# Attention out of its branch, one branch for the expert slots with the usual arm laid last (RWKV attention with top-1 experts, one Trainium2 core)

## The chip, the cores and the metric

The kernel runs on one core of a Trainium2 chip. The metric is the time of one execution on the device in microseconds (us), the median of several runs. Engines are called PE (TensorE), DVE (VectorE), ACT (ScalarE), POOL (GpSimd) and SP (SyncE); each runs its own program, and a branch stands in all five programs.

## The reference

An RWKV attention over 4 batches, 8 heads, 768 tokens of 48 elements, and then a layer of 8 experts, of which each of the 3072 tokens takes the best one (384 elements in, 1024 between).

```
for t in range(S):
    cur = einsum('bhd,bhe->bhde', u * k[t], v[t])
    y[t] = einsum('bhd,bhde->bhe', r[t], state + cur)
    state = w[:, :, None] * state + einsum('bhd,bhe->bhde', k[t], v[t])
x = y, as 3072 x 384
logits = x @ w_gate;  e_idx = argmax(logits)
gate_w = softmax(logits)[e_idx];  eom = sigmoid(x @ w_output_gate)
for e in range(8):
    h = maximum(x[e_idx == e] @ w1[e], 0)
    out[e_idx == e] = gate_w * eom[:, e] * (h @ w2[e])
```

w lies between 0.85 and 0.95 in the inputs that are timed.

## The kernel before

**Head.** Constants are made, w and u are loaded by `load_heads` on SP's queue (four small loads), and r, k and v of the first chunks too. `make_flag` and `read_flag` find out whether all w are between 0.6 and 1.6; the result is `flag`, read into a register of each engine at line 1178. `make_powers` computes powers of w for one chunk.

**Attention.** It is computed in 24 chunks of 128 tokens. That holds for w near 1; the branch at line 1234 on `flag` has this chunked form as its first arm (the fall-through), and in its second arm `slow_attention`, which goes token by token. `Attention.first` transposes r and k of the first chunk (`ps_f`) and multiplies them by the powers (`RT`, `KT`), `prep` multiplies those of later chunks (`Rn`, `Kn`), `product` makes `P`. While PE works on chunk i, the router works on chunk i - 1 and finds each token's expert and its place in it. The order of all instructions in this part is that of the code (`manual_schedule`). After the arm's last instruction each engine jumps over the other arm; the place where they meet is called the join here.

**Experts.** Expert slots 0 to 7 are worked one after the other. A slot has two layers: `l1` (lines 799 to 801, three products of high and low halves in fp32r, into `ps_h`; `l1_out` makes `hh` on ACT and `hl` on DVE from it) and layer 2 (`l2_step`, lines 861 to 863, into `ps_o`). `gather` (line 770, an indirect DMA on POOL) fetches a slot's tokens into `xg`; `xt` (line 782) transposes them into `ps_xt` and splits them. `split1` and `split2` split weights into halves, `load1` and `load2` fetch the next ones. `scatter` scales the rows (`yo`) and writes them with an indirect DMA on POOL (line 836). The first 256 columns of slot 0 are worked at the end of the attention (`early_rest`), the other 256 behind the join: `run` orders their eight pieces of `l1` by hand, with the rest of the router's last work among them (among it the small table `ps_tab`); then `layer2(0, ...)`, outside the manual order, so that a scheduler places its matmuls, and the gathers' transposes and the weights of slot 1 with them.

**Levels.** How many rows of each expert are computed is a table, `CAPS[n]`. `level` (line 905) is a branch on the number that the router found: level 0 is the usual one and the first arm (the fall-through); two more arms follow, and behind the first one each engine jumps over them. Last, at line 1368, a branch on `ovf` around `overflow`, which computes tokens that found no place; here it has none.

The functions that the change touches:

Of the kernel before, what the change touches and what calls it, by code (L numbers as in the profile page):

```python
# [19 lines left out]
C = 128  # L20
# [26 lines left out]
WARM = (4, 0, 0, 0, 1, 3)  # L47
# [157 lines left out]
class Attention:  # L205
    def __init__(self, tc, ctx, k, load, x_d):
        self.tc, self.k = tc, k
        self.load, self.x_d = load, x_d
        self.pw = ctx.enter_context(tc.tile_pool(name="att_w", bufs=2))
        self.T = None  # L210
        self.st, self.vc, self.A = {}, {}, [None, None]
        self.Rn, self.Kn = ([self.pw.tile([C, H, HB], F32, name=f"{nm}{i}", bufs=1) for i in range(n)] for nm, n in (("Rn", 2), ("Kn", 3)))
# [12 lines left out]
    def first(self, ps):  # L225
        nc, k = self.tc.nc, self.k
        ts = self.load(0)
        RK = [None, None]
        for n in (1, 0):
            p = ps.tile([C, NP, C], F32, name="ps_f", tag="at", bufs=2)  # L230
            warm_up(self.tc, k, WARM[2 + n])
            for q in range(NP):
                nc.tensor.transpose(p[:, q, :], k.raw0["rk"[n]][:, 2 * q : 2 * q + 2, :], k.ident)
            RK[n] = self.pw.tile([C, NP, C], F32, name=("RT", "KT")[n])
            nc.vector.tensor_mul(RK[n], p, (k.pr, k.pk)[n])
        self.st[0] = [None, None, ts[2]] + RK

    def product(self, i):
# [3 lines left out]
        self.P = self.pw.tile([C, NP, C], F32, name="P", bufs=1)  # L242
# [15 lines left out]
    def trans(self, ps, i):  # L258
# [4 lines left out]
        RT = self.pw.tile([C, NP, C], F32, name="RT")  # L263
        KT = self.pw.tile([C, NP, C], F32, name="KT")
# [78 lines left out]
class Router:  # L343
    def __init__(self, tc, pool, k, wg, wog):
# [22 lines left out]
        self.level = pool.tile([1, 1], I32, name="level")  # L367
        self.ovf = pool.tile([1, 1], I32, name="ovf")
# [315 lines left out]
    def finish(self, w, tot):  # L684
# [28 lines left out]
        yield V  # L713
        nc.vector.tensor_copy(self.level, lvl)


class Experts:
    def __init__(self, tc, ctx, k, rt, w1, w2, x_d, out):
# [8 lines left out]
        self.xg = [p.tile([QP, DM], F32, name=f"xg{q}") for q in range(NQ)]  # L727
        self.ys, self.ph = {}, {}
# [98 lines left out]
    def scatter(self, s, q, p, pool=None):  # L827
        nc = self.tc.nc
        n = self.rows(s, q)
        yo = (pool or self.op).tile([QP, DM], F32, name=f"yo{q}")  # L830
# [44 lines left out]
    def early_rest(self, ps, pool):  # L875
# [5 lines left out]
        for q in range(EARLY):  # L881
# [7 lines left out]
            self.scatter(0, q, p, pool)  # L889
        self.gather(1, range(self.nq(1)))  # L890

    def run(self, rest):
        with self.tc.manual_schedule(engines=ORDERED):
            for f in range(FC):
# [500 lines left out]
```

## Time and profile before

| | |
|---|---|
| median of 3 runs | 400.09 us (400.07 to 401.25) |
| profiled execution | 400.7 us |
| its span | 399.0 us |
| granted clock of PE, mean | 0.981 |

The span is the time from the first to the last instruction of the profiled execution; 1.7 us of its time lie outside. All times of rows count from the span's start. A granted clock of 1.00 is 2.4 GHz, and 0.50 is 1.2 GHz.

### The profile page before, as it was taken

The page shows a single profiled execution, that of the slowest core. Times are in us where ns is not written, and L with a number is a line of the kernel's source. Part 1 is how long each engine was busy: PE and PEld are TensorE (multiplying, and loading weights), DVE is VectorE, ACT ScalarE, POOL GpSimd, SP SyncE. Part 2 cuts the span into 40 slices and gives each one's busy share as a digit, 9 for nine tenths or more (in the row PEclk, how much of TensorE's full clock was granted, in tenths as well). Part 3 has the DMA queues.
Part 4 walks back from the last instruction along what each step waited for, and adds up shares of the span by engine and source line. Part 5 has one row for each costly group of instructions (what it writes and reads, how often), then busy time and mean ns, then how long its engine had stood idle before and what let it go on. Part 6 is the DMA issues. An engine that isn't in the chain of part 4 may idle for free. (4 is left out here: it accounts for less than half of the span.)

```text
span 399.0 us, 12122 instructions
## 1 busy us (share of the span) xinstructions
PE 368.8 (92%) x5004; PEld 350.6 (88%) x5004; DVE 229.8 (58%) x516; ACT 150.5 (38%) x303; POOL 122.0 (31%) x170
## 2 busy tenths in 40 slices
PE   6899999999898989689999999999999999999960
PEld 3799989998787888689989999999999999999960
DVE  5776797678888648347651652662654636625200
ACT  2233323333243452134542652653634626525200
POOL 6423234232346772241501331232224216010020
PEclk9999999999999999979999999999999999999995
DMA  7976776775987320743371751751852935620010
GB/s 124 189 153 143 164 151 131 160 161 121 222 216 185 102 81 2 222 134 120 120 245 39 221 178 46 220 176 50 257 162 77 284 106 166 209 82 17 2 60 5
DMA packets 104970, 54.87 MB, mean 138 GB/s; under 512 B 78911, under 2 KB 102515, under 8 KB 104896
## 3 DMA queue, kind: packets, MB, share of 16 engines
q1 hardware_dynamic: 101472, 44.08, 42.9%
q0 software_dynamic: 3424, 9.82, 7.5%
q8 instruction: 44, 0.72, 0.8%
q14 instruction: 30, 0.25, 0.2%
HBM read 44.45 MB, written 9.76 MB: 136 GB/s over the span
## 5 line engine op out<-in xcount | busy, mean ns | idle before, releaser
L799 PE MATMUL ps_h<-xh,w1h 128*128 128x384 f32 (+4 forms) x216 | 73.5, 340 | 4.7 <-issue 4.1
L800 PE MATMUL ps_h<-xl,w1h 128*128 128x384 f32 (+4 forms) x216 | 71.7, 332 | 0.0
L801 PE MATMUL ps_h<-xh,w1l 128*128 128x384 f32 (+4 forms) x216 | 71.7, 332 | 0.0
L836 POOL DMA_INDIRECT out_dram<-yo,si x28 | 28.8, 1028 | 135.0 <-ACT yo L833 72.8
L243 POOL TENSOR_TENSOR P<-RT,KT 128x512 f32<-128x512 f32 x24 | 30.8, 1283 | 72.7 <-ACT xT L379 45.2
L809 DVE SCALAR_TENSOR_TENSOR hl<-ps_h,hh 128x384 fp32r<-128x384 f32 (+4 forms) x72 | 37.9, 532 | 18.1 <-ACT hh L808 17.7
L808 ACT ACTIVATE hh<-ps_h 128x384 fp32r<-128x384 f32 (+4 forms) x72 | 33.9, 473 | 37.8 <-PE ps_h L801 36.0
L799 PEld LDWEIGHTS ps_h<-xh,w1h 128*128 128x128 f32 x216 | 41.8, 194 | 5.7 <-issue 4.4
L770 POOL DMA_INDIRECT xg<-x_d,gi x28 | 31.2, 1114 | 45.8 <-PE ps_xt L782 30.0
L861 PE MATMUL ps_o<-w2h,hh 128*128 128x384 f32 x128 | 43.5, 340 | 0.0
L863 PE MATMUL ps_o<-w2h,hl 128*128 128x384 f32 x128 | 42.9, 335 | 0.0
L862 PE MATMUL ps_o<-w2l,hh 128*128 128x384 f32 x128 | 42.8, 334 | 0.0
L800 PEld LDWEIGHTS ps_h<-xl,w1h 128*128 128x128 f32 x216 | 41.8, 194 | 0.1
L801 PEld LDWEIGHTS ps_h<-xh,w1l 128*128 128x128 f32 x216 | 41.7, 193 | 0.2
L748 DVE TENSOR_TENSOR w1l<-raw,w1h 128x768 fp32r<-128x768 f32 x28 | 26.7, 955 | 22.8 <-ACT w1h L747 22.8
L285 DVE TENSOR_TENSOR A<-ps_a,mask 128x512 f32<-128x512 f32 x48 | 30.8, 683 | 10.1 <-PE ps_a L281 9.9
L747 ACT CAST w1h<-raw 128x768 fp32r<-128x768 f32 (+1 forms) x36 | 27.1, 763 | 25.1 <-PE ps_h L800 20.0
L785 DVE TENSOR_TENSOR xl<-ps_xt,xh 128x384 fp32r<-128x384 f32 (+4 forms) x27 | 13.6, 536 | 30.5 <-ACT xh L784 30.2
L748 DVE TENSOR_TENSOR w2l<-raw,w2h 128x768 fp32r<-128x768 f32 x28 | 26.7, 960 | 7.4 <-ACT w2h L747 5.7
L269 ACT COPY KT<-ps_t 128x512 f32<-128x512 f32 x23 | 13.5, 587 | 44.0 <-PE ps_t L268 40.6
L747 ACT CAST w2h<-raw 128x768 fp32r<-128x768 f32 (+1 forms) x36 | 26.9, 764 | 7.2 <-PE ps_o L863 2.8
L281 PE MATMUL ps_a<-RT,KT 64*64 64x128 f32 x768 | 26.9, 276 | 0.9 <-DVE vc L255 0.8
(217 smaller groups left out, 698.0 us busy)
## 6 DMA issues: line engine op xcount, KB each, us to landing
raw<-in_moe_w_dram SPq DMA_DIRECT2D x64, 384.0 KB, 3.6
x_d<-x SPq DMA_DIRECT2D x24, 192.0 KB, 3.6
v_t<-in_v_dram SPq DMA_DIRECT2D x21, 192.0 KB
k_t<-in_k_dram SPq DMA_DIRECT2D x20, 192.0 KB, 3.6
r_t<-in_r_dram SPq DMA_DIRECT2D x20, 192.0 KB, 4.2
raw<-in_v_dram SPq DMA_DIRECT2D x3, 192.0 KB, 3.6
raw<-in_k_dram SPq DMA_DIRECT2D x3, 192.0 KB, 3.1
xg<-x_d,gi POOLq DMA_INDIRECT x28, 4.4
```

The source lines that it names most:

```text
L243: self.tc.nc.gpsimd.tensor_mul(self.P, RT, KT)
L747: nc.scalar.copy(hi, self.raw[i][:, cs])
L748: (eng or nc.vector).tensor_sub(lo, self.raw[i][:, cs], hi)
L770: nc.gpsimd.indirect_dma_start(out=self.xg[q][:n], out_offset=None, in_=self.x_d[:n_x, :], in_offset=bass.IndirectOffsetOnAxis(ap=self.rt. ...
L799: nc.tensor.matmul(o, wh[:, j, fs], xh, start=(j == 0), stop=False)
L800: nc.tensor.matmul(o, wh[:, j, fs], xl, start=False, stop=False)
L801: nc.tensor.matmul(o, wl[:, j, fs], xh, start=False, stop=(j == KC - 1))
L808: nc.scalar.activation(hh, o, AF.Relu)
L809: nc.vector.scalar_tensor_tensor(hl, o, 0.0, hh, op0=ALU.max, op1=ALU.subtract)
L861: nc.tensor.matmul(o, hh, wh, start=(f == 0), stop=False)
L862: nc.tensor.matmul(o, hh, wl, start=False, stop=False)
L863: nc.tensor.matmul(o, hl, wh, start=False, stop=(f == FC - 1))
```

## The change

The chunked attention stands in no arm any more: every execution runs it. One branch is left on the usual path, behind layer 2 of slot 0, on `rare`, which is the level plus `slow` (1 where w is out of bounds, the opposite of the old flag). Its usual arm computes slots 1 to 7 with `CAPS[0]` and is laid behind the rare arm (`preferred_fallthrough_block=False`), so that it is the taken side and the program's last part. The rare arm computes the attention and slot 0 again token by token, if `slow` is set, chooses the table, and ends with the overflow. A hint names the branch at the start of each engine's program. To make this possible, tiles of the attention and the early outputs move to pools that stay, memsets and the first transposes move ahead, the flag of w goes by DVE and POOL, w and u are loaded on ACT's queue, and layer 2 of slot 0 is ordered by hand (`bridge`). Two more lists of numbers change: where warm-up matmuls stand, and after which chunks weight pieces are split.

```diff
-WARM = (4, 0, 0, 0, 1, 3)
+WARM = (4, 3, 1)
@@ load_heads
-        tc.nc.sync.dma_start(t[HB * j : HB * j + D], src.rearrange("(q j) d -> j d q", j=2)[j])
+        tc.nc.scalar.dma_start(t[HB * j : HB * j + D], src.rearrange("(q j) d -> j d q", j=2)[j])
@@ read_flag
+    k.slow = pool.tile([1, 1], F32, name="slow")
+    nc.vector.tensor_scalar(k.slow, low, float(C) - 0.5, None, op0=ALU.is_lt)
     k.flag = pool.tile([1, 1], I32, name="flag")
-    nc.vector.tensor_scalar(k.flag, low, float(C) - 0.5, None, op0=ALU.is_ge)
+    nc.gpsimd.tensor_copy(k.flag, k.slow)
@@ Router.finish
+        nc.vector.tensor_add(self.rare, lvl, k.slow)
         nc.vector.tensor_copy(self.level, lvl)
@@ Experts
+    def run(self, rest, rare):
+        tc = self.tc
+        with tc.manual_schedule(engines=ORDERED):
+            tc.mark_branch_hint_location("level", "LikelyTaken", engines=tuple(ORDERED))
+            self.late(rest)
+        fit = tc.nc.values_load(self.rt.rare[0:1, 0:1], min_val=0, max_val=NL + 1)
+        with tc.If(fit == 0, label="level", preferred_fallthrough_block=False) as cmp:
+            self.slots(CAPS[0])
+        with cmp.Else():
+            rare()
+
+    def late(self, rest):
+        for f in range(FC):
+            self.l1(f, EARLY * QP, self.caps[0], self.ps, *(("at", 2), ("u", 1), ("at", 2), ("y", 1))[f % 4])
+            for _ in range(REST):
+                next(rest, None)
+        for _ in rest:
+            pass
+        self.bridge()
-        self.layer2(0, list(range(EARLY, self.nq(0))))
-        self.level(self.tc.nc.values_load(self.rt.level[0:1, 0:1], min_val=0, max_val=NL), 0)
+    def bridge(self):
+        for j in range(KC):
+            self.xt(1, j, list(range(self.nq(1))), self.ps, "uyg"[j], 1)
+        e = self.reg(1)
+        for i, q in enumerate(range(EARLY, self.nq(0))):
+            p = self.ps.tile([C, 512], F32, name="ps_o", tag="tr", bufs=2)
+            for f in range(FC):
+                self.l2_step(0, q, p, f)
+            self.scatter(0, q, p)
+            for n in range(2 * i, 2 * i + 2):
+                self.split1(n)
+                self.load2(e, n)
@@ rwkv_top1_moe
             sums = make_flag(tc, const, ps, k)
+            att = Attention(tc, hctx, k, load, x_d)
+            att.first(ps)
+            warm_up(tc, k, WARM[1])
             make_powers(tc, rw, k, lambda: read_flag(tc, const, sums, k))
+            load(2)
+            att.scaled()
+            make_tables(tc, ps, k)
+            warm_up(tc, k, WARM[2])
+            for a in PRE:
+                att.prep(*a)
+            att.product(0)
             make_caps(tc, const, k)
-            load(2)
-        warm_up(tc, k, WARM[5])
-        fast = nc.values_load(k.flag[0:1, 0:1], min_val=0, max_val=1)
...
-        with tc.If(fast == 1) as cmp:
-            with ExitStack() as fctx:
...
-                    for _ in range(SPLITS if i >= SPLIT_AT else 0):
+                for _ in range(SPLITS if SPLIT_AT <= i < NT - 1 else 0):
...
-        with cmp.Else():
-            with ExitStack() as sctx:
+        with ExitStack() as mctx:
+            ex.start(mctx, ps)
...
+            def rare():
+                again = nc.values_load(k.flag[0:1, 0:1], min_val=0, max_val=1)
+                with tc.If(again == 1):
+                    with ExitStack() as sctx:
+                        redo(sctx)
+                ex.higher(nc.values_load(rt.level[0:1, 0:1], min_val=0, max_val=NL), 0)
+                more = nc.values_load(rt.ovf[0:1, 0:1], min_val=0, max_val=1)
+                with tc.If(more == 1):
+                    with ExitStack() as octx:
+                        overflow(tc, octx, ps, k, ex, x_d, w2, out)
+
+            ex.run(prog, rare)
```

The order of instructions shows it at three places. First SP's queue at the head, from its first load on (`raw` tiles hold r, k or v of later chunks, `wt` and `ut` are w and u); before, and then with the change:

```order
L200 DMA k_117<-in_k_dram 128x8x48
L77 DMA wt<-in_w_dram 48x4x1 [waits DVE_49]
L77 DMA wt<-in_w_dram 48x4x1
L200 DMA r_119<-in_r_dram 128x8x48
L200 DMA raw_68<-in_v_dram 128x8x48
L77 DMA ut<-in_u_dram 48x4x1 [waits DVE_49]
L77 DMA ut<-in_u_dram 48x4x1
L200 DMA raw_68<-in_k_dram 128x8x48
L200 DMA raw_69<-in_r_dram 128x8x48 [waits DMAHW0_49]
L200 DMA raw_69<-in_v_dram 128x8x48 [waits DMAHW1_49]
L349 DMA wg_153<-in_moe_w_gate_dram 128x3x8 [waits DMAHW2_49]
```

```order
L1438 BRANCH_PREFETCH_HINT
L202 DMA k_119<-in_k_dram 128x8x48
L202 DMA r_121<-in_r_dram 128x8x48
L202 DMA raw_68<-in_v_dram 128x8x48
L202 DMA raw_68<-in_k_dram 128x8x48
L202 DMA raw_69<-in_r_dram 128x8x48 [waits DMAHW0_49]
L202 DMA raw_69<-in_v_dram 128x8x48 [waits DMAHW1_49]
L355 DMA wg_155<-in_moe_w_gate_dram 128x3x8 [waits DMAHW2_49]
L356 DMA wg_155<-in_moe_w_output_gate_dram 128x3x8 [waits DMAHW3_49]
```

The four loads of `wt` and `ut` are gone from the queue, and everything behind them moves up by two to four places.

Second, PE behind the fourth of eight pieces of the late layer 1 (xh, xl, w1h, w1l are halves of slot 0's tokens and weights; hh and hl of its hidden values; `ps_tab` is the router's small table). Before:

```order
L800 MATMUL ps_h<-xl_93,w1h_74 128x256
L801 MATMUL ps_h<-xh_92,w1l_75 128x256
L861 MATMUL ps_o<-w2h_80,hh_94 128x384
L862 MATMUL ps_o<-w2l_81,hh_94 128x384
L863 MATMUL ps_o<-w2h_80,hl_95 128x384
L861 MATMUL ps_o<-w2h_80,hh_96 128x384
L862 MATMUL ps_o<-w2l_81,hh_96 128x384
L863 MATMUL ps_o<-w2h_80,hl_97 128x384
L531 MATMUL ps_tab<-last_rhs,last_ohp 64x32 x16
L799 MATMUL ps_h<-xh_88,w1h_76 128x256
```

and with the change:

```order
L809 MATMUL ps_h<-xl_93,w1h_74 128x256
L810 MATMUL ps_h<-xh_92,w1l_75 128x256
L538 MATMUL ps_tab<-last_rhs,last_ohp 64x32 x16
L808 MATMUL ps_h<-xh_88,w1h_76 128x256
L809 MATMUL ps_h<-xl_89,w1h_76 128x256
L810 MATMUL ps_h<-xh_88,w1l_77 128x256
```

The six matmuls of layer 2 (lines 861 to 863) that stood ahead of the table are gone from there.

Third, PE between that layer 1 and the branch. With the change, the last of the 12 transposes of slot 1's tokens (line 791, the old 782) are followed by the first of layer 2 (lines 870 to 872, the old 861 to 863):

```order
L791 MATMUL ps_xt<-ident,xg_110 128x128
L791 MATMUL ps_xt<-ident,xg_111 128x128
L791 MATMUL ps_xt<-ident,xg_112 128x128
L791 MATMUL ps_xt<-ident,xg_113 128x80
L870 MATMUL ps_o<-w2h_80,hh_94 128x384
L871 MATMUL ps_o<-w2l_81,hh_94 128x384
L872 MATMUL ps_o<-w2h_80,hl_95 128x384
```

In the kernel before, the first transposes stood only ahead of the last matmul of layer 2's first row:

```order
L861 MATMUL ps_o<-w2h_86,hh_108 128x384
L862 MATMUL ps_o<-w2l_87,hh_108 128x384
L782 MATMUL ps_xt<-ident,xg_110 128x128
L782 MATMUL ps_xt<-ident,xg_111 128x128
L863 MATMUL ps_o<-w2h_86,hl_109 128x384
L782 MATMUL ps_xt<-ident,xg_112 128x128
L782 MATMUL ps_xt<-ident,xg_113 128x80
```

So the 12 transposes have moved from the middle of layer 2 to its front, directly behind layer 1's last piece. Behind layer 2 both programs have the load and the branch; in the changed one slot 1 is not the next row:

```order
L870 MATMUL ps_o<-w2h_86,hh_108 128x384
L871 MATMUL ps_o<-w2l_87,hh_108 128x384
L872 MATMUL ps_o<-w2h_86,hl_109 128x384
L906 TENSOR_LOAD rare
L907 COMPARE_AND_BRANCH
L1406 TENSOR_LOAD flag
L1407 COMPARE_AND_BRANCH
```

What stands behind the branch there is the rare arm; slot 1's layer 1 has moved behind it, to the program's end.

## Rows read from the trace of the kernel before

**Rows 1.** Page, busy time, share of the span and instructions of each engine

```profile
PE 368.8 (92%) x5004; PEld 350.6 (88%) x5004; DVE 229.8 (58%) x516; ACT 150.5 (38%) x303; POOL 122.0 (31%) x170
```

**Rows 2.** Windows: stretch, length, busy us (count) by engine, granted clock, DMA share, GB/s

```profile
10.00:20.00 10.00, 8.38 (x217) 7.63 (x217) 7.74 (x14) 2.53 (x5) 4.38 (x6) 1.00 0.94 189
20.00:30.00 10.00, 9.89 (x286) 9.24 (x283) 7.09 (x14) 3.26 (x8) 2.82 (x5) 1.00 0.71 153
...
165.00:170.00 5.00, 1.52 (x11) 1.17 (x9) 1.74 (x4) 0.75 (x2) 0.99 (x1) 0.85 0.67 234
170.00:175.00 5.00, 4.42 (x20) 4.42 (x21) 0.89 (x5) 0.73 (x2) 3.78 (x5) 0.50 0.49 140
```

**Rows 3.** Timeline of SP's queue: start, duration in us, then what [idle before]

```profile
1.29 1.06 SPq L77 DMA_DIRECT2D wt<-in_w_dram  x2
...
3.50 1.46 SPq L77 DMA_DIRECT2D ut<-in_u_dram  x2
...
9.00 0.58 SPq L200 DMA_DIRECT2D raw<-in_r_dram  x1
```

**Rows 4.** Timeline of DVE at the head

```profile
7.50 0.69 DVE L235 TENSOR_TENSOR KT<-ps_f,pk_t 128x512 f32<-128x512 f32 x1 [0.37 <-PE ps_f L233]
...
12.52 0.56 DVE L222 TENSOR_TENSOR Rn<-raw,PR 128x384 f32<-128x384 f32 x1 [1.13 <-DMA raw<-in_r_dram]
```

**Rows 5.** Timeline of PE at the join, and later

```profile
166.19 0.34 PE L863 MATMUL ps_o<-w2h,hl 128*128 128x384 f32 x1
170.58 0.58 PE L799 MATMUL ps_h<-xh,w1h 128*128 128x256 f32 x1 [4.05 <-issue]
...
175.22 0.33 PE L799 MATMUL ps_h<-xh,w1h 128*128 128x256 f32 x1
...
176.95 0.28 PE L801 MATMUL ps_h<-xh,w1l 128*128 128x256 f32 x1
...
178.21 1.12 PE L531 MATMUL ps_tab<-last_rhs,last_ohp 128*64 128x32 f32 x32
...
203.62 0.46 PE L799 MATMUL ps_h<-xh,w1h 128*128 128x424 f32 x1 [0.60 <-DVE hl L809]
```

**Rows 6.** Source view of two branch lines: durations in ns, first and last start

```profile
L1234 PEldq COMPARE_BRANCH  x2: 84/2585/5086, 6.3 to 165.4; - x2
...
L905 PEldq COMPARE_BRANCH  x2: 87/1661/3235, 189.8 to 382.5; - x2
```

**Rows 7.** Timeline of DVE and POOL, join and end

```profile
166.79 0.61 DVE L835 TENSOR_SCALAR yo<-ps_o,sc 128x384 f32<-128x384 f32 x1
169.01 1.01 POOL L836 DMA_INDIRECT out_dram<-yo,si  x1 [5.63 <-DMA out_dram<-yo,si]
173.32 0.42 DVE L809 SCALAR_TENSOR_TENSOR hl<-ps_h,hh 128x256 fp32r<-128x256 f32 x1 [5.92 <-ACT hh L808]
174.29 0.97 POOL L770 DMA_INDIRECT xg<-x_d,gi  x1 [0.30 <-DMA xg<-x_d,gi]
...
386.66 0.98 POOL L836 DMA_INDIRECT out_dram<-yo,si  x1 [3.14 <-ACT yo L833]
```

**Rows 8.** DMA view, issues: count, KB each, median us from issue to landing

```profile
raw<-in_moe_w_dram SPq DMA_DIRECT2D x64, 384.0 KB, 3.6
...
xg<-x_d,gi POOLq DMA_INDIRECT x28, 4.4
out_dram<-yo,si POOLq DMA_INDIRECT x28, 2.6
```

**Rows 9.** Source view of the last branch line and the end, on POOL

```profile
L1368 POOLq COMPARE_BRANCH  x1: 55/55/55, 390.1 to 390.1; - x1
L1368 POOLq INC_SWDGE_SEM  x1: 1312/1312/1312, 392.1 to 392.1; - x1
...
L1391 POOLq EVENT_SEMAPHORE  x4: 17/17/17, 398.2 to 398.9; - x4
L1391 POOLq DRAIN  x3: 46/111/4648, 393.5 to 398.7; - x3
```

More of the change, by code (lines that the diff above doesn't have):

```diff
@@ L367, in __init__ @@
         self.level = pool.tile([1, 1], I32, name="level")
+        self.rare = pool.tile([1, 1], I32, name="rare")
         self.ovf = pool.tile([1, 1], I32, name="ovf")
@@ L727, in __init__ @@
         self.xg = [p.tile([QP, DM], F32, name=f"xg{q}") for q in range(NQ)]
+        self.yo = [p.tile([QP, DM], F32, name=f"yo_e{q}") for q in range(EARLY)]
         self.ys, self.ph = {}, {}
@@ L888, in early_rest, with settle, higher @@
                     yield
-            self.scatter(0, q, p, pool)
+            self.scatter(0, q, p, self.yo[q])
         self.gather(1, range(self.nq(1)))
-    def run(self, rest):
-        with self.tc.manual_schedule(engines=ORDERED):
-            for f in range(FC):
-                self.l1(f, EARLY * QP, self.caps[0], self.ps, *(("at", 2), ("u", 1), ("at", 2), ("y", 1))[f % 4])
-                for _ in range(REST):
-                    next(rest, None)
-            for _ in rest:
-                pass
-        self.layer2(0, list(range(EARLY, self.nq(0))))
-        self.level(self.tc.nc.values_load(self.rt.level[0:1, 0:1], min_val=0, max_val=NL), 0)
-    def level(self, fit, n):
+    def run(self, rest, rare):
[16 more added lines that the diff above has]
+        self.bridge()
+    def settle(self):
+        nc = self.tc.nc
+        for t in self.yo:
+            nc.gpsimd.memset(t, 0.0)
+        for q in range(EARLY, self.nq(0)):
+            for _ in range(2):
+                nc.gpsimd.memset(self.op.tile([QP, DM], F32, name=f"yo{q}"), 0.0)
+    def higher(self, fit, n):
         if n < NL:
@@ L928, in layer2 @@
                     self.load2(e, n)
-                for j in ((), (0, 1, 2), (), ())[i] if s else range(KC * (i == 0)):
+                for j in ((), (0, 1, 2), (), ())[i]:
                     self.xt(s + 1, j, list(range(self.nq(s + 1))), self.ps, "uyg"[j], 1)
@@ L1005, in slow_attention, with overflow @@
             )
-def overflow(tc, ctx, k, rt, x_d, w1, w2, out):
+def overflow(tc, ctx, ps, k, ex, x_d, w2, out):
     nc = tc.nc
+    rt = ex.rt
     pool = ctx.enter_context(tc.tile_pool(name="ovf", bufs=1))
-    wk = ctx.enter_context(tc.tile_pool(name="ovf_w", bufs=2))
-    ps = ctx.enter_context(tc.tile_pool(name="ovf_ps", bufs=1, space=PSUM))
-    w1_v = w1.rearrange("e (j p) f -> e p j f", p=C)
+    wk = ctx.enter_context(tc.tile_pool(name="ovf_w", bufs=1))
     w2_v = w2.rearrange("e (f p) d -> e p f d", p=C)
@@ L1097, in overflow @@
         e = nc.sync.value_load(esi[0:1, bass.ds(j, 1)], min_val=0, max_val=E - 1)
-        a = pool.tile([C, KC, F], F32, name="o_w1")
         b = pool.tile([C, FC, DM], F32, name="o_w2")
-        nc.sync.dma_start(a, w1_v[bass.ds(e, 1)].rearrange("a p j f -> p (a j) f"))
+        for i in range(4):
+            ex.load1(e, i)
         nc.sync.dma_start(b, w2_v[bass.ds(e, 1)].rearrange("a p f d -> p (a f) d"))
@@ L1346, in rwkv_top1_moe, with redo @@
+        hctx.close()
+        with ExitStack() as mctx:
+            ex.start(mctx, ps)
+            def redo(sctx):
+                ex.settle()
                 slow_attention(tc, sctx, ps, k, r, kk, v, w, u, x_d)
@@ L1360, in rwkv_top1_moe @@
                 ex.early_mm(ps, 1)
-                for _ in ex.early_rest(ps, rw):
+                for _ in ex.early_rest(ps):
                     pass
-        with ExitStack() as mctx:
-            ex.start(mctx, ps)
-            ex.run(prog)
+                ex.late(prog)
+            def rare():
[9 more added lines that the diff above has]
+            ex.run(prog, rare)
     pctx.close()
-    more = nc.values_load(rt.ovf[0:1, 0:1], min_val=0, max_val=1)
-    with tc.If(more == 1):
-        with ExitStack() as octx:
-            overflow(tc, octx, k, rt, x_d, w1, w2, out)
 _INS = ["r", "k", "v", "w", "u", "moe_w_gate", "moe_w_output_gate", "moe_w1", "moe_w2"]
```

231 lines of the change are left out of this document (114 added, 117 removed).

## The prediction

> **What bounds the kernel now.** I read the page's busy times first: TensorE (PE) works 92% of the span [rows 1], so a change pays only where PE stands still, where its clock is low, or after its last matmul. The windows show where that is [rows 2]. In the steady part (20 to 30 us) PE is busy 9.89 of 10 us. Three places stand out: the head (8.38 of 10 us between 10 and 20), the stretch from 165 to 175 us, where PE is busy 1.52 of 5 us and then runs 5 us at a granted clock of 0.50, and the end, where POOL's last transfer is issued by 387.64 us [rows 7] and POOL closes the span after 398.9 [rows 9]. I then looked at each place in the timeline, and at the branch lines by source. All three places have a branch of the program in them.
>
> **The join of the attention's two arms.** PE's last matmul of the fast arm starts at 166.19 and the first of what follows at 170.58, with 4.05 us of idle time that no releaser explains ("issue") [rows 5]. The source view says what it was: the jump over the slow arm (line 1234, second execution) held PE's sequencer for 5086 ns, from 165.4 us [rows 6]. The sequencer runs ahead of the array, so about 1 of the 5.09 us is hidden. After the gap, the matmuls start 0.211 us apart (22 steps from 170.58 to 175.22, 4.64 us), then 0.124 apart (14 steps to 176.95) [rows 5]; the granted clock in that stretch is 0.50 [rows 2], the lower of the clock's two levels (1.2 against 2.4 GHz), and what PE did before it fell was to stand still. The slow steps cost 22 x (0.211 - 0.124) = 1.9 us; I take 2.0 with the first matmul's start. In the changed kernel nothing lies between these matmuls, so **-4.05 - 2.0 = -6.05**. The bounds are -5.0, if something else of what follows is late by up to 1 us, and -6.1. Its inputs are there: the only one late in the row is the PSUM buffer that the first scatter's scaling frees, which DVE starts at 166.79 [rows 7], and the next matmul group uses another buffer.
>
> **The head.** SP loses the four small w and u loads, 1.06 + 1.46 us of issue time [rows 3], and the load of the flag with its branch. The four go to ACT's queue, ahead of a table load; ACT is 38% busy [rows 1]. The raw r load of the third chunk, issued at 9.00 [rows 3], stands behind the w and u loads and ahead of the flag, so it can start up to 2.5 us earlier; its landing ended DVE's 1.13 us wait at 12.52, and the first product, at 7.50, was 0.37 late behind PE's transposes [rows 4], which now stand ahead of the flag and the powers. 1.13 + 0.37 = 1.5; with 0.3 for the w load, which no longer stands behind SP's first issue, I take **-1.8**. The ends are -0.9 (transfers share the bandwidth, so an issue 2.5 us earlier lands much less earlier) and -2.6 (all of SP's 2.52). The steady part is bound by PE, so a head that ends earlier moves everything behind it. The moved weight pieces at the end of the attention I cost at 0, because the same pieces are only spread differently; 0.5 either way.
>
> **The bridge.** The 72 late matmuls of layer 1 now run at 0.12 us each from the start, so what feeds their followers has less time. Before, the scheduler had put six matmuls of layer 2 ahead of the last small table and the rest ahead of the transposes of slot 1. Now the table's 16 pairs stand right behind the fourth of eight pieces, and the 12 transposes ahead of all of layer 2. The transposes need three PSUM buffers, and one of them comes free only when the last piece has gone through ACT and DVE: 0.42 us on DVE [rows 7] and as much on ACT, of which the array's own tail hides a little, 0.6 us of wait. The table waits for a chain on DVE that began at 173.32 with the first piece [rows 7] and has half the time now: 0.4. The last gather of slot 1 started at 174.29; in its queue it stands behind a scatter that started at 169.01, though DVE's share of its input was ready at 166.79 + 0.61 = 167.4 [rows 7]. So it starts between 172.7 and 174.3 on the old axis, and lands 4.4 us later by the page's median [rows 8], at 177.1 to 178.7. It is needed at 166.4 + 72 x 0.12 + 1.05 for the table [rows 5], 176.1, plus the 1.0 of the two waits: 0 to 1.6 us more. I take **+1.0** for the bridge (0 to +2.6). The pieces of slot 1's weights are split after the first layer 2 row instead of as early as the scheduler liked, and the loads of the next weights follow them: four at 3.6 us [rows 8] are 14.4 us if one waits for the other, against the second layer 2 row and slot 1's first layer, which follows the level's branch of 189.8 [rows 6] and still runs at 203.62 [rows 5]. That covers them within about 1 us.
>
> **The branch on rare.** It takes the place of the level's branch, which fell through and held PE's sequencer for 87 ns [rows 6]. Now the usual arm is on the taken side, behind the whole rare arm. The code names this branch to the fetcher with a hint, and no row of before shows an executed hint on such a branch. The lower bound is the fall-through, **+0.1**; the upper one is the join again, +6.05, and a shorter jump (line 905's second on PE, 3235 ns) would give 4.05 - (5.09 - 3.24) = 2.2 us of idle time and at most 2.0 of low clock. I take the lower one, since the branch has a hint and PE has about 160 us of straight code to use it in.
>
> The Trainium skill, Runtime: NRT & Kernel Launch, section Instruction fetch mechanics, says that prefetch is purely sequential and that a taken branch whose target is not in the current window of two pages forces a fetch before execution can go on. The join's 5086 ns agrees with it [rows 6]. By that rule alone the usual arm's move to the taken side costs what the join cost, and the sum would be 395.0; by the row of the fall-through it is 389.0. The page says nothing of hints.
>
> **The end.** POOL's last scatter starts at 386.66 and takes 0.98 us [rows 7]. Then POOL comes over two jumps: behind the end of the level's arms, and behind the overflow's test at 390.1, and starts to clear its queue's semaphores at 392.1 [rows 9]. After it stand 1.31 us, a drain of 4.65 us, and the last barrier at 398.9. With the usual arm laid last, nothing is jumped: 392.1 - 387.64 = 4.5 us, less about 0.15 for the branches that remain, **-4.3**. The lower bound is -2.9, if POOL must wait until the scatter has landed (2.6 us after its start [rows 8], 389.3). It assumes that the drain keeps its length. Nothing else is late then: PE, ACT and DVE have no work there.
>
> **The sum.** -6.05 - 1.8 + 0 + 1.0 + 0.1 - 4.3 = -11.05. The profiled execution took 400.7 us with a span of 399.0 and 1.7 us around it; the median is 0.6 lower at 400.09. The span should become 387.95, the profiled execution 389.65, and the median 400.09 - 11.05 = 389.0.
>
> **The rivals.**
> - The hint does nothing for PE. All else is the same: 389.0 + 5.95 = 395.0, and 391.1 to 393.1 for the shorter jump. For it: the far jumps of before held PE's sequencer for 3.2 and 5.1 us [rows 6]. Against it: only the hint, which before did not have.
> - The end or the head gives nothing. The drain on POOL ends with something other than POOL's own work, and grows by what went before it: +4.3, 393.3. Or the third chunk's r lands when it did: +1.8, 390.8. Against the first: the scatter has landed at 389.3, four microseconds before the drain starts.
> - Slower than before: the hint, standing second in each engine's program, takes the fetcher away from the straight code ahead of the branch, at the cost of a late fetch for each stretch of PE's code. Its price is a far jump, 3.2 us or more for each; the gain of 11.05 is gone at the fourth (11.05 / 3.2 = 3.5), and a dozen of them would give 389.0 + 38 = 427. For it, only that the hint comes so early. Against it: a fetcher that follows one branch has no reason to drop the straight line.
>
> **How the numbers follow.** Forecast 0.67 (389.0, its own range 386.4 to 392.5: the worst terms together give -0.9 + 0.5 - 5.0 + 2.6 + 0.1 - 2.9 = -5.6, 394.5, the best -2.6 - 0.5 - 6.1 + 0.1 - 4.5 = -13.6, 386.5, and not all the bad ones fall together); the hint idle 0.17; end or head without gain 0.09; still better than 386.4, 0.03; slower 0.03; a mix that ends at the old time 0.01. The range of 386.4 to 395.2 takes in the first three. A difference of 0.3% (1.2 us) is about what a measurement of this kernel can tell from none: faster 0.95, same 0.02, slower 0.03.
>
> **What would show it.** The clock granted stays at 1.00 from 160 to 180 us and PE has no gap above 0.5 us before the late layer 1; the wait at the 12 transposes is under 2 us; PE's sequencer spends about 0.1 us, not 3 to 5, at the branch on rare, and slot 1 follows layer 2 without a gap; POOL's clearing starts within 0.3 us of the last scatter's end, and from that end to the span's end there are about 6.9 us (now 11.4); DVE's third Rn starts near 10.7 instead of 12.52. Wrong would be: a 4 us gap at slot 1 with a half clock after it, a drain longer than 4.65 us, gaps marked "issue" in the attention.

## The result: 1% faster, where 2.8% was forecast

The changed kernel takes 396.56 us (median of 8 runs, 395.56 to 398.71), the kernel before 400.84 beside it (8 runs; one of 519.82 is left out of the comparison, and the other seven have a median of 400.43). The ratio to those seven is 0.9903, 95% interval 0.9876 to 0.993. The forecast was 389.0 and the range 386.4 to 395.2, so the sign was right and the size was not: the gain is about 4 us, not 11.

The profiled execution's span is 395.6 us against 399.0. The page's busy times of the changed kernel answer to [rows 1] and say little, since the work is the same:

```profile
PE 370.5 (94%) x5004; PEld 352.9 (89%) x5004; DVE 231.9 (59%) x517; ACT 150.1 (38%) x303; POOL 122.4 (31%) x171
```

Its windows, which answer to [rows 2], say where the time lies (columns as there: stretch, length, busy us and count of PE, PE's weight loads, DVE, ACT and POOL, granted clock, DMA share, GB/s):

```profile
155.00:160.00 5.00, 3.60 (x53) 3.39 (x52) 3.92 (x15) 0.47 (x2) 0.41 (x1) 0.88 0.01 3
160.00:165.00 5.00, 5.00 (x25) 5.00 (x24) 2.44 (x13) 0.58 (x1) 1.65 (x2) 0.78 0.48 121
165.00:170.00 5.00, 5.00 (x35) 4.90 (x34) 1.72 (x4) 1.12 (x4) 1.03 (x1) 1.00 0.88 312
170.00:175.00 5.00, 4.58 (x62) 4.32 (x60) 3.04 (x12) 1.63 (x5) 3.26 (x4) 1.00 0.25 82
...
195.00:200.00 5.00, 1.43 (x8) 1.05 (x7) 2.81 (x5) 2.40 (x4) 3.39 (x4) 0.98 0.66 209
200.00:205.00 5.00, 4.95 (x18) 4.38 (x17) 2.20 (x4) 2.51 (x5) 0.00 (x0) 0.68 0.88 287
```

The gap of the join is gone: PE is busy 5.00 and 4.58 of 5 us from 165 to 175, at full clock, where it had 1.52 and then a clock of 0.50. But there are two new holes, in stretches that were full in the kernel before:

```profile
155.00:160.00 5.00, 5.00 (x65) 4.83 (x64) 3.37 (x18) 0.58 (x2) 1.46 (x2) 1.00 0.03 7
195.00:200.00 5.00, 5.00 (x28) 4.86 (x27) 4.26 (x7) 2.46 (x4) 3.78 (x5) 1.00 0.77 230
```

With the change, PE is busy only 3.60 us from 155 to 160, with a lower clock behind it (0.78). From 195 to 200 it is busy only 1.43 us, and the clock is at 0.68 after that. PE's timeline names what it waited for:

```profile
157.14 1.12 PE L538 MATMUL ps_tab<-last_rhs,last_ohp 128*64 128x32 f32 x32 [1.40 <-DVE last_rhs L528]
...
174.06 1.12 PE L538 MATMUL ps_tab<-last_rhs,last_ohp 128*64 128x32 f32 x32 [0.42 <-DVE last_rhs L532]
...
180.84 1.02 PE L791 MATMUL ps_xt<-ident,xg 128*128 128x128 f32 x8 [0.75 <-DVE hl L818]
...
199.03 0.46 PE L808 MATMUL ps_h<-xh,w1h 128*128 128x424 f32 x1 [3.57 <-DVE hl L818]
```

The four waits are for the table of the early pieces (1.40 us, DVE), for the small table of the bridge (0.42) and the last piece through DVE (0.75), which the prediction had named, and for a PSUM buffer in slot 1's first layer (3.57). None of them is marked "issue" as the 4.05 us of [rows 5] are. The source view of the line of the branch on rare (ns: shortest, median and longest of two, first and last start) shows what the hinted branch took of PE's sequencer:

```profile
L907 PEldq COMPARE_BRANCH  x2: 191/292/392, 187.6 to 385.1; - x2
```

It is 0.39 us or less, where the jump of [rows 6] had taken 5.09. A gap of some 4 us at slot 1 with a lower clock behind it is what the prediction had named as the sign of an idle hint; the 3.57 us at 199.03 look like it, but they begin 5.4 us behind slot 1's first matmul and end with DVE, not with the branch.

The end became shorter by more than forecast. POOL's last scatter in the timeline, and then the source view of the end:

```profile
389.08 0.98 POOL L845 DMA_INDIRECT out_dram<-yo,si  x1 [3.14 <-POOLq L907]
```

```profile
L1438 POOLq EVENT_SEMAPHORE  x4: 17/17/17, 394.8 to 395.5; - x4
L1438 POOLq DRAIN  x3: 46/115/5519, 389.2 to 395.3; - x3
```

From the last scatter's end (390.06) to the last barrier (395.5) it is 5.4 us, against 11.3 by [rows 7, 9]. The step of 1.31 us ahead of the drain is no longer there, and the drain is 5.52 us long because it begins at 389.2, while the scatter is still being issued; 4.66 of it lie behind the scatter's end, as much as the whole drain took before (4.65). A drain longer than 4.65 us was among the prediction's signs of being wrong; here it only starts earlier.

To see where the time went I read the same six places in each trace: A, the start of the last three transposes for the logits (in the kernel before at 145.42); B, the first matmul of slot 0's early layer 2; C, the first of its late layer 1; D, the first of slot 1 (424 columns); E, the first of slot 2 (408 columns); F, the last matmul. The table gives A and then the distances, all in us of the profiled executions.

| kernel | A | A to B | B to C | C to D | D to E | E to F | F to span's end |
|---|---|---|---|---|---|---|---|
| before | 145.42 | 11.63 | 13.53 | 21.86 | 30.68 | 162.31 | 13.54 |
| changed | 145.83 | 12.58 | 10.64 | 21.03 | 35.52 | 162.24 | 7.71 |
| difference | +0.4 | +0.95 | -2.9 | -0.8 | +4.8 | -0.1 | -5.8 |

The sum is -3.4, the difference of the spans. Forecast were -1.8, 0, -6.05 and +1.0 for A to D, +0.1 and -4.3.

### The profile page after: what moved, and what is told of

Same layout as the page of the kernel before. It is cut to its first block, busy times and chain, and to the rows that moved or that the text cites. A ratio compares the mean times of both kernels' runs of the same rounds, so it can differ in the third digit from the quotient of the medians.

```text
span 395.6 us, 12084 instructions
## 1 busy us (share of the span) xinstructions
PE 370.5 (94%) x5004; PEld 352.9 (89%) x5004; DVE 231.9 (59%) x517; ACT 150.1 (38%) x303; POOL 122.4 (31%) x171
## 5 line engine op out<-in xcount | busy, mean ns | idle before, releaser
L845 POOL DMA_INDIRECT out_dram<-yo,si x26 | 26.6, 1023 | 123.4 <-ACT yo L842 76.6
```

## The experiments

All times are medians beside the kernel before on the same chip; the ratio is to that. The kernel before took 400.84 us beside the changed kernel, and 402.12, 401.54 or 401.43 beside those below. So two kernels that did not run beside each other, as the changed one and those below, are compared by their times to about 1 us only; the distances A to F are the finer measure, each from one execution.

**The weights of slot 1.** In the changed kernel the four loads of slot 1's second weights leave SP's queue from 188.50 on (before: 176.51), as they stand behind `split1`, and that behind the first layer 2 row. SP's timeline shows it, before and then with the change:

```profile
176.51 10.04 SPq L740 DMA_DIRECT2D raw<-in_moe_w_dram  x4
```

```profile
188.50 4.62 SPq L749 DMA_DIRECT2D raw<-in_moe_w_dram  x4
```

ACT's timeline shows who pays, before and then with the change:

```profile
189.77 1.66 ACT L747 CAST w2h<-raw 128x768 fp32r<-128x768 f32 x2 [0.42 <-DVE xl L785]
191.63 0.83 ACT L747 CAST w2h<-raw 128x768 fp32r<-128x768 f32 x1 [0.20 <-PE ps_o L863]
194.43 0.53 ACT L808 ACTIVATE hh<-ps_h 128x424 fp32r<-128x424 f32 x1 [1.96 <-PE ps_h L801]
```

```profile
192.05 0.84 ACT L756 CAST w2h<-raw 128x768 fp32r<-128x768 f32 x1 [2.37 <-DMA raw<-in_moe_w_dram]
...
193.49 0.83 ACT L756 CAST w2h<-raw 128x768 fp32r<-128x768 f32 x1 [0.61 <-DMA raw<-in_moe_w_dram]
...
196.64 0.83 ACT L756 CAST w2h<-raw 128x768 fp32r<-128x768 f32 x1 [2.32 <-DMA raw<-in_moe_w_dram]
197.38 0.52 ACT L817 ACTIVATE hh<-ps_h 128x424 fp32r<-128x424 f32 x1
```

In both kernels three splits of those weights (`w2h`) stand in ACT's queue ahead of slot 1's first hidden values (`hh`). Before, none of them waited for its load; now each does: 2.37, 0.61 and 2.32 us. The first `hh` comes at 197.38, though its nine matmuls had ended by 192; PE has no PSUM buffer left after the third group and stands still for 3.57 us, with the clock at 0.68 from 200 to 205. Two kernels test it. The first splits, and loads, ahead of layer 2's rows:

```diff
         e = self.reg(1)
+        for n in range(4):
+            self.split1(n)
+            self.load2(e, n)
         for i, q in enumerate(range(EARLY, self.nq(0))):
...
             self.scatter(0, q, p)
-            for n in range(2 * i, 2 * i + 2):
-                self.split1(n)
-                self.load2(e, n)
```

> The changed kernel with the four weight pieces of slot 1 split, and the next loads issued, ahead of layer 2's rows instead of behind them. Theory: PE's 3.57 us gap at 199.03 and the half clock behind it come from the loads of the second weights, issued 12 us later than before, for which ACT's queue waits ahead of the hidden values; issued some 4 us earlier, the gap falls to under 1 us and the kernel gains 3 to 4.8 us (391.8 to 393.6). Rival: the gap is the price of the taken branch or of something on DVE; it stays above 2.5 us and the gain is under 1 us.

Measured: 391.39 us, ratio 0.9729 (0.9687 to 0.9771). D to E is 30.53, as before the change; one wait of PE, of 0.42 us, is left there. The second leaves the loads late and orders slot 1's layer 1 by hand:

```diff
+            octx = ExitStack()
+            if s == 1:
+                octx.enter_context(self.tc.manual_schedule(engines=ORDERED))
...
-                if f % 2 == 0:
-                    self.split2(f // 2)
+                n = f - 3 if s == 1 and 3 <= f < 7 else f // 2 if s > 1 and f % 2 == 0 else -1
+                if n >= 0:
+                    self.split2(n)
                     if more:
-                        self.load1(e, f // 2)
+                        self.load1(e, n)
...
+            octx.close()
```

> The changed kernel with slot 1's layer 1 ordered by hand: the splits of its second weights stand behind the fourth to seventh hidden values, the loads stay as late as they are. Theory: late loads alone do no harm; what does is that two to three splits that wait for them stand ahead of the first hidden values in ACT's queue. With the order turned round the 3.57 us gap goes and the kernel gains 2 to 4 us (392.6 to 394.6), with some of it given back at the next weights, which are split later. Rival: the loads are late for their own users too, and layer 2 of slot 1 waits instead; the gain is under 1 us.

Measured: 391.49 us, ratio 0.9732 (0.9683 to 0.978), D to E 30.03. So the late loads do no harm by themselves, and the order in ACT's queue did none before; together they make PE wait. Both gained more than the theory said (5.2 and 5.1 us against the changed kernel's 396.56, where it had 3 to 4.8 and 2 to 4), and nothing was given back at the next weights: E to F is 162.24 in all three.

**The weight pieces at the attention's end.** This kernel splits them where the kernel before did:

```diff
-                for _ in range(SPLITS if SPLIT_AT <= i < NT - 1 else 0):
+                for _ in range(SPLITS if i >= SPLIT_AT else 0):
...
+            while pieces:
+                weights0(pieces.pop(0))
             dst, prog = slot(NT - 1)
...
-                elif pieces:
-                    weights0(pieces.pop(0))
```

> The changed kernel with the weight pieces split where they were before (two behind each chunk from 18 to 23, the last four ahead of the last logits). Theory: six pieces among the router's last work put POOL's subtractions (148.86 to 154.7 us) beside DVE's chain, which slows both; DVE's operations there take their old times (0.21 to 0.23 instead of 0.44 to 1.04 us), PE is busy over 9.2 of 10 us from 150 to 160 again and keeps a granted clock of 1.00 there, and the kernel gains 1.8 to 2.6 us (394.0 to 394.8). Rival: DVE's chain is late for another reason, DVE's times stay long or PE's gap at the table stays, and the gain is under 0.7 us.

Measured: 394.94 us, ratio 0.9825 (0.9774 to 0.9875). A to B is 11.64, the old value, and B to C 9.10. The gain is 1.6 us by the times, a little under the theory's 1.8 to 2.6, and 2.5 from A to C. And the other way round, the kernel before with these lines alone as the change has them:

> The kernel before, with nothing changed but the last six weight pieces, which stand among the router's last work. Theory: POOL's six subtractions move to 148.9 to 154.7 us and DVE's operations beside them take 0.4 to 1.0 us instead of 0.2; from the last transpose for the logits to the first layer 2 matmul 12.3 to 12.4 us instead of 11.41, and 1.5 us more where the clock falls behind PE's gap: 0.9 to 2.5 us slower. Rival: the slow operations are the changed kernel's alone, and the time stays within 0.5 us.

Measured: 402.58 us against 401.43, ratio 1.003 (1.0002 to 1.0057), A to B 12.59: the 0.95 us are there again, and the clock did not fall behind that gap this time. DVE's timeline of the changed kernel in the chain behind the logits:

```profile
150.84 1.04 DVE L429 TENSOR_TENSOR last_oh<-sc,m 128x64 f32<-128x64 f32 x1
...
152.14 0.21 DVE L487 TENSOR_TENSOR rk<-ps_c,base 128x64 f32<-128x64 f32 x1
152.38 0.48 DVE L489 TENSOR_TENSOR rk<-rk,last_oh 128x64 f32<-128x64 f32 x1
...
153.36 0.44 DVE L501 TENSOR_TENSOR ge<-rank,thr 128x32 f32<-128x32 f32 x1
...
154.06 0.69 DVE L509 SCALAR_TENSOR_TENSOR pp<-q,rank 128x8 f32<-128x8 f32 x1
```

POOL's at the same time:

```profile
148.86 5.87 POOL L757 TENSOR_TENSOR w2l<-raw,w2h 128x384 fp32r<-128x384 f32 x6 [6.01 <-ACT w2h L756]
```

And DVE's with the pieces back in their place, the same operations in the same order:

```profile
151.80 0.21 DVE L429 TENSOR_TENSOR last_oh<-sc,m 128x64 f32<-128x64 f32 x1
152.34 0.22 DVE L487 TENSOR_TENSOR rk<-ps_c,base 128x64 f32<-128x64 f32 x1
152.59 0.22 DVE L489 TENSOR_TENSOR rk<-rk,last_oh 128x64 f32<-128x64 f32 x1
...
153.32 0.18 DVE L501 TENSOR_TENSOR ge<-rank,thr 128x32 f32<-128x32 f32 x1
...
153.76 0.17 DVE L509 SCALAR_TENSOR_TENSOR pp<-q,rank 128x8 f32<-128x8 f32 x1
```

While POOL subtracts (`w2l`, six times about 1 us from 148.86 on), four of DVE's operations with two operands in SBUF take 1.04, 0.48, 0.44 and 0.69 us instead of 0.2; the one that reads PSUM (`rk<-ps_c`) takes 0.21 and 0.22. Each of the four ends 0.02 to 0.08 us behind the end of one of POOL's six, as if it had waited for that; in the kernel before with these lines alone it is the same. ACT's halves of the pieces moved too, but they had ended by 151.54, and three of the four start later. The Trainium skill, SBUF — State Buffer, Who interferes with whom, states that a VectorE instruction with two inputs in SBUF contends with a GpSimd instruction that reads SBUF, as its second input comes over a port that the two share. The trace agrees: the longest of the four, 1.04 us, is about the length of one of POOL's instructions (1.01 to 1.03).

**The branch.** From the version with early splits (391.39) the hint's line is taken out:

```diff
-            tc.mark_branch_hint_location("level", "LikelyTaken", engines=tuple(ORDERED))
```

> The version with early splits (391.4), without the hint on the branch. Theory: the hint is what makes the taken branch cheap; without it PE's sequencer stands 3 to 5 us at the branch (0.39 us with it), PE is idle 2 to 4 us ahead of slot 1, and 1.5 to 2 us go to the lower clock: 395.4 to 397.5. Rival: the branch was cheap for another reason; PE's sequencer stays under 1 us and the time within 0.7 us of 391.4.

Measured: 396.96 us, ratio 0.9883 (0.984 to 0.9926). The source view of the branch line:

```profile
L906 PEldq COMPARE_BRANCH  x2: 185/3372/6558, 188.0 to 385.6; - x2
```

And PE's timeline at slot 1's first matmul, then ACT's behind the branch:

```profile
194.83 0.69 PE L808 MATMUL ps_h<-xh,w1h 128*128 128x424 f32 x1 [4.16 <-ACT w2h L756]
```

```profile
192.65 2.30 ACT L756 CAST w2h<-raw 128x768 fp32r<-128x768 f32 x3 [5.48 <-issue]
```

The taken branch without its hint holds PE's sequencer for 6.56 us, longer than any jump of [rows 6]. C to D grows from 21.02 to 25.36. (The idle time is put down to ACT's `w2h`, but slot 1's first matmul does not read that; PE's sequencer was at the branch from 188.0 to 194.6, and PE starts 0.3 us behind it.) ACT also stands still behind the branch, for 5.48 us. The rule on taken branches of the Trainium skill, Runtime: NRT & Kernel Launch, Instruction fetch mechanics, agrees with the 6.56 us here and not with the 0.39 us of the hinted branch, of which it says nothing.

Then the same version without the hint, and with the usual arm laid first:

```diff
-        with tc.If(fit == 0, label="level", preferred_fallthrough_block=False) as cmp:
+        with tc.If(fit == 0, label="level", preferred_fallthrough_block=True) as cmp:
```

> The version with early splits (391.4), with the usual arm laid first, as the level's arms were before, and no hint, so that the branch falls through and the rare arm is jumped over at the end. Theory: the branch costs nothing either way, and the end gets its jump back: from the last scatter's start to the span's end 9 to 11 us instead of 6.47, so 394.0 to 396.0. Rival: the end was long because of the second branch, on the overflow, and not because of the jump; then the end stays under 7.5 us and the time within 1 us of 391.4.

Measured: 392.87 us, ratio 0.978 (0.9751 to 0.981). That is 1.5 us more than with early splits alone, between the theory's 2.6 to 4.6 and the rival's 1. C to D is 21.03, so the branch on rare costs nothing when it falls through. F to the span's end is 10.21 instead of 7.71. POOL's last scatter in the timeline, and the source view of the drain:

```profile
383.24 0.98 POOL L845 DMA_INDIRECT out_dram<-yo,si  x1 [3.66 <-POOLq L906]
```

```profile
L1437 POOLq DRAIN  x3: 50/107/4702, 386.2 to 391.4; - x3
```

From the last scatter's start to the span's end (391.7) it takes 8.46 us, again between the theory's 9 to 11 and the rival's 7.5. The drain starts some 2 us behind the scatter's end and has its old length, so the jump over the rare arm costs 2.0 us behind the scatter's start; another 0.5 lies ahead of it, and no run shows why. Of the 5.8 us that the change gained at the end, about 2.0 come from where the usual arm lies; the other 3.8, by subtraction, go with the second branch, on the overflow, which is no longer passed. From that branch at 390.1 to the drain at 393.5 it was 3.4 us in the kernel before, the 1.31 us step among them [rows 9].

**The head.** Three kernels. In the changed kernel DVE's chain begins with w, in this row of its timeline, and the third Rn (the one of the third chunk) waits for nothing:

```profile
5.87 0.17 DVE L135 TENSOR_SCALAR ok<-wt 128x4 f32<-128x4 f32 x1 [4.26 <-DMA wt<-in_w_dram]
...
14.43 0.55 DVE L226 TENSOR_TENSOR Rn<-raw,PR 128x384 f32<-128x384 f32 x1
```

Before, w was used at 4.29 and the third Rn came at 12.52 [rows 4]. In the first kernel `load_heads` is on SP's queue again:

```diff
-        tc.nc.scalar.dma_start(t[HB * j : HB * j + D], ...
+        tc.nc.sync.dma_start(t[HB * j : HB * j + D], ...
```

> The changed kernel with the four loads of w and u back on SP's queue. Theory: in the changed kernel w lands late because its tiny transfers on ACT's queue meet the big ones of SP (DVE's first use of wt at 5.87 us against 4.29), and all of the head hangs on w; on SP's queue the first use is again at 4.3 to 4.6, the third Rn (14.43 in the changed kernel) comes 1.0 to 1.6 us earlier, and the whole kernel gains 0.4 to 1.5 us against the changed one's 396.56. Rival: the late start comes from the new order of the head (transposes and memsets ahead), then wt lands early but the third Rn stays at 14 or later and the time stays within 0.4 us.

Measured: 396.43 us, ratio 0.9864 (0.9824 to 0.9904), A at 146.21. The first use of w moved to 4.41 and the third Rn to 12.95, as the theory has it; the time stayed, as the rival has it (by the ratios, 0.9864 against 0.9903, it may have gained, but their intervals overlap). The second also moves the three warm-up matmuls of the middle to the start:

```diff
-WARM = (4, 3, 1)
+WARM = (7, 0, 1)
```

> The changed kernel with w and u on SP's queue (396.43), and the three warm-up matmuls moved from behind the first transposes to the start (7, 0, 1). Theory: the three stand in PE's way for 1.3 us, and the first 16 transposes run at 0.22 us each instead of 0.115 as PE has done too little before; so the first Kn comes 1.2 us earlier (8.7 instead of 9.97). The third r still lands at 12.5 to 13, so the third Rn moves by less than 0.4 and the time by less than 0.6: the forecast's gain from an earlier r does not exist, since the transfers share the bandwidth. Rival: with all engines earlier the third Rn comes at 11.5 or before and the kernel gains 1 us or more against 396.43.

Measured: 396.40 us, ratio 0.9887 (0.9836 to 0.9939), A at 146.28. DVE's timeline:

```profile
8.80 0.55 DVE L226 TENSOR_TENSOR Kn<-k,PK 128x384 f32<-128x384 f32 x1
...
11.29 1.27 DVE L291 TENSOR_TENSOR A<-ps_a,mask 128x512 f32<-128x512 f32 x2
12.97 1.68 DVE L226 TENSOR_TENSOR Rn<-raw,PR 128x384 f32<-128x384 f32 x1 [0.41 <-DMA raw<-in_r_dram]
```

The first Kn came at 8.80, but the third Rn waits for r again, 0.41 us. The third is the kernel before with w and u on ACT's queue, the first diff of this part the other way round:

> The kernel before, with nothing changed but the four loads of w and u, which go to ACT's queue. Theory: w lands 1 to 1.6 us later among the large transfers (first use of wt at 5.3 to 5.9 instead of 4.29), the flag and the powers with it, and the first transpose of the logits (17.55) moves to 18.3 to 19: the time rises by 0.7 to 1.5 us. SP's loads start up to 2.5 us earlier in the list, but the third r is issued less than 1 us earlier. Rival: SP's queue was what held the head; the third Rn comes before 12.0 and the time falls by 0.5 us or more.

Measured: ratio 1.0011 (0.998 to 1.0042), A at 146.41, 1 us later than before. DVE's timeline at the head:

```profile
5.61 0.17 DVE L135 TENSOR_SCALAR ok<-wt 128x4 f32<-128x4 f32 x1 [4.09 <-DMA wt<-in_w_dram]
...
9.05 0.69 DVE L235 TENSOR_TENSOR KT<-ps_f,pk_t 128x512 f32<-128x512 f32 x1 [0.57 <-PE ps_f L233]
...
14.99 0.55 DVE L222 TENSOR_TENSOR Rn<-raw,PR 128x384 f32<-128x384 f32 x1
```

And SP's, the third r:

```profile
8.22 0.58 SPq L200 DMA_DIRECT2D raw<-in_r_dram  x1
```

w is used at 5.61 instead of 4.29, though its loads are issued at 0.96 us, ahead of the 1.29 of [rows 3]; the third r is issued at 8.22, 0.8 us earlier than there and not 2.5. The loss of 1 us at A is in the trace of one execution; the times (401.49 us against 401.43 beside it) do not tell it from no change, and the theory's 0.7 to 1.5 us are not there.

**All of it undone.** Early splits, the pieces, w and u, and the warm-up matmuls together, the rest of the change kept:

> The changed kernel with all the suspected losses undone together: w and u on SP's queue, weight pieces split where they were before, slot 1's splits and loads ahead of layer 2's rows, and the three warm-up matmuls back at the start (7, 0, 1). Theory: the three places are independent, so from the 391.4 of the version with early splits 0.95 (the pieces) and, where the clock fell behind that gap, 1.5 more come off, and 0.4 to 1.5 at the head: 387.5 to 389.6, which is the forecast of the change as it was meant. Rival: the losses overlap (what one step gives, the next wait takes), and it stays above 390.5.

Measured: 389.30 us (387.55 to 392.18), ratio 0.9708 (0.9668 to 0.9748). This is the fastest of all. A is at 146.54; then 11.64, 9.10, 21.03, 29.50, 162.24 and 7.71. Two attempts to better it:

> The version with the four losses undone (389.3), with slot 1's transposes behind the first row of layer 2, as before the change, instead of ahead of it. Theory: the wait of 0.44 us for the PSUM buffer goes, and from the late layer 1 to slot 1 it takes 20.3 to 20.6 us instead of 21.03: 388.6 to 389.0. Rival: the split halves of slot 1's tokens then come too late and slot 1 waits for them, as much or more; 389.3 or above.

The edit, on top of that version:

```diff
     def bridge(self):
-        for j in range(KC):
-            self.xt(1, j, list(range(self.nq(1))), self.ps, "uyg"[j], 1)
...
             self.scatter(0, q, p)
+            for j in range(KC * (i == 0)):
+                self.xt(1, j, list(range(self.nq(1))), self.ps, "uyg"[j], 1)
```

Measured: 390.55 us, ratio 0.9723 (0.9681 to 0.9766). The times of the two overlap (the version of 389.3 has 387.55 to 392.18, this one 389.05 to 392.54). C to D is 20.97, so no more than 0.06 was gained there, and D to E is 30.74 instead of 29.50, with a wait of 0.47 us for DVE in slot 1: the rival.

> The version with the four losses undone (389.3), with the two loads of the gates' weights moved behind the third chunk's loads on SP's queue. Theory: what the third r waits for is the transfers ahead of it, not SP's time; with two of them out of its way it lands 0.5 to 1.3 us earlier, DVE's wait of 0.84 us ahead of the third Rn goes, and the first transpose for the logits comes at 17.1 to 17.6 instead of 17.93: 388.5 to 389.1. Rival: these two are too small to matter (12 KB each), Rn and the time stay within 0.2 us.

The edit moves the two loads of the gates' weights:

```diff
-        nc.sync.dma_start(self.wg32[:, :, :E], ...
-        nc.sync.dma_start(self.wg32[:, :, E : 2 * E], ...
...
             load(2)
+            nc.sync.dma_start(rt.wg32[:, :, :E], ...
+            nc.sync.dma_start(rt.wg32[:, :, E : 2 * E], ...
             att.scaled()
```

Measured: 392.85 us (389.89 to 394.77), ratio 0.9762 (0.9716 to 0.9807). The head did what the theory said (A is at 145.67, 0.9 earlier), but C to D is 24.83. DVE's timeline, at the head and later:

```profile
12.76 0.55 DVE L226 TENSOR_TENSOR Rn<-raw,PR 128x384 f32<-128x384 f32 x1
...
176.52 0.19 DVE L544 TENSOR_TENSOR tab<-tab,ps_tab 128x32 f32<-128x32 f32 x1 [4.59 <-remote]
```

ACT's:

```profile
176.62 0.94 ACT L815 ACTIVATE hh<-ps_h 128x256 fp32r<-128x256 f32 x3 [5.15 <-remote]
```

The third Rn comes at 12.76 with no wait. At 176.5 DVE and ACT both wake from 4.6 and 5.2 us of idle time, though PE's records show its matmuls running. What held PE's signals back there is open.

## Why the prediction missed

- **The join**: right. Of its 6.05 us, 4.05 lie between B and C, and that distance fell by 4.43 us wherever the clock stayed up (9.08 to 9.18 in nine kernels); in the changed kernel's own profile 1.55 of it were lost to a lower clock behind the new gap at 157. The 2.0 of slow steps lie between C and D. The prediction counted 22 slow steps of 0.211 us; there are 21, of 0.221, which gives the same 2.0.
- **The end**: right in kind, too small: -5.8 against -4.3. The term kept the 1.31 us step ahead of the drain, which is gone, and let the drain start behind the scatter, where it starts with it.
- **The branch on rare**: right. With the hint 0.39 us of sequencer and no gap; the rival's 4 us gap came when the hint went.
- **The bridge**: right as far as the term went. C to D is 21.03; before it was 21.86, of which 2.0 were lost to the half clock, so +1.17 against +1.0. The waits of 0.42 and 0.75 us are those that were named.
- **The weights of slot 1**: the step that failed most. The prediction put this at nothing: it said that the late loads were covered "within about 1 us" by the second layer 2 row and slot 1's first layer. It counted when the weights are needed, by layer 2 of slot 1, and not who stands behind the waiting instruction: the splits wait in ACT's queue ahead of the hidden values of layer 1. It cost 4.8 us, 3.57 of them a wait of PE and the rest behind it at the lower clock.
- **The moved pieces**: costed at 0 "because the same pieces are only spread differently". They moved POOL's work beside a chain on DVE that PE waits for; that cost 0.95 us, and 1.55 more where the clock fell.
- **The head**: forecast -1.8, measured +0.4 in the profile at A. Two steps failed. The first is "so it can start up to 2.5 us earlier": the third r was issued 0.6 to 0.8 us earlier, because the nine other loads ahead of it took longer to issue, 6.6 us in all instead of 5.2, and SP waited 0.5 us between two of them. It landed 3.4 us after its issue, at 11.8 instead of about 12.5, so some 0.7 of the 1.13 us of wait would have gone. But the chain on DVE ahead of it was later: w, with which it begins, came 1.1 to 1.6 us later on ACT's queue, where the prediction had it 0.3 earlier. The second is "a head that ends earlier moves everything behind it". From the first transpose for the logits to A it takes 127.3 to 129.9 us by profile, so the head's microsecond is not what arrives at A: the kernel with the gates' weights moved had that transpose 1.7 us earlier than the changed kernel (16.83 against 18.57) and A 0.2 earlier. A lies between 145.7 and 148.3 in all eleven kernels with the changed head, against 145.42 and 145.53 in the two with the old one as it was. The changed kernel and the one with slot 1 ordered by hand, whose heads are alike, are 2.4 us apart there. What makes the difference on the way is open.

In the changed kernel's profile these add up: the head 2.2 us short of its forecast, the pieces 0.95 and 1.55, the weights 4.8, less 1.5 that the end gave more, make 8.0 us, where 7.6 lie between -11.05 and -3.4: the other terms together came out 0.4 better than forecast.

With the splits, the pieces, w and u and the warm-up undone the kernel takes 389.3 us, close to the 389.0 that were forecast for the change as a whole. That is partly chance: the end gave 1.5 more than its term and D to E 1.2 that no term held, and in place of the head's -1.8 A is 1.1 later in that profile. What the branches cost was read rightly; what the change moved beside them was not.

## What to carry to other kernels

When a transfer is issued later, look not only at when its data is needed but at the queue in which its consumer waits: what stands behind that instruction is late too. When work is moved "for nothing", look at which engine runs beside it at the new place; POOL's subtractions beside a chain of DVE's operations with two operands in SBUF cost some of them up to a whole POOL instruction here. A far branch that is taken in the usual case costs PE 4 us of idle time here, and almost nothing if a hint names it ahead of time; a kernel that ends behind a far jump pays 2.0 to 2.5 us for it.

## What the runs showed that was not expected

- The same gap of PE at 157 us (A to B of 12.58 to 12.60 in eight kernels) was followed by the lower clock in two of them (B to C of 10.64 and 10.68) and not in the other changed ones (9.08 to 9.11).
- A far jump to code that no hint names took PE's sequencer 3.24 us and 5.09 [rows 6] and 6.56, by kernel and place.
- The head's first transposes ran at half the rate: 1.09 us for four in the changed kernel, 0.63 in the kernel before and in the version of 389.3 us. The windows show a granted clock of 1.00 there, but they count a stretch without a record as 1.00, and the trace's record of the clock begins only at 12.03 us in the changed kernel (4.66 in the kernel before, 5.00 in the version of 389.3). The rate doubles where the record begins; in the kernel of 396.40, with seven warm-up matmuls, that is at 6.79, as PE's timeline shows:

```profile
5.41 1.09 PE L236 MATMUL ps_f<-ident,k 128*128 128x128 f32 x4
6.30 0.85 PE L236 MATMUL ps_f<-ident,r 128*128 128x128 f32 x4
7.55 0.66 PE L188 MATMUL ps_pw<-ident,pk_t 128*128 128x128 f32 x4 [0.40 <-DVE pk_t L174]
```

So up to there the head ran at the rate of the lower clock. That need not be the change's doing: in the kernel before with only the pieces moved, whose head is the old one, the record begins at 12.34 and the first four took 1.09 too.
